# Loading four chunks ahead of the weights, transposing by DMA, and smaller first blocks in a fused retention and feed-forward kernel

## The chip, the core and the metric

The kernel runs on one core of a Trainium2 chip. The metric is device microseconds (us) from the first to the last instruction of the program, median over several executions. A program on one core is called "slow" here when it is over 1.5% above the fastest run of the same kernel; comparisons use fast runs. Every experiment was run in rounds with the kernel before on the same chip. Its medians in the rounds were 226.49, 225.42, 226.47 and 226.48 us, so differences between rounds of up to 1 us are not read as effects.

The engines are PE (matrix multiply, with PEld for its weight loads), DVE (vector), ACT (activation), POOL, and SP, which issues all DMA transfers of this kernel, in program order. Every engine is given its instructions in the order that the program fixed.

## The reference

Two stages. The first is a retention layer: 4 batches, 8 heads, 768 steps, head dimension 64. The second is a feed-forward layer with a squared ReLU on 3072 tokens.

```python
for t in range(S):                               # q, k, v: (4, 8, 768, 64) f32
    state = gamma * state + k[t] (x) v[t]        # per batch and head, 64 x 64
    y[t]  = scale * q[t] @ state
x = y.transpose(0, 2, 1, 3).reshape(3072, 512)
h = maximum(x @ w_in, 0)                         # w_in: 512 x 2048
out = (h * h) @ w_out                            # w_out: 2048 x 512
```

## The kernel before

The 768 steps of a batch are cut into 6 chunks of 128 steps, 24 chunks in all. For a chunk, k, q and v are loaded as f32 (256 KB each, in rows of 256 bytes), cast to bf16, and k and q are transposed. A "visit" on PE then computes the scores of a new chunk and the outputs of the chunk before it, from 64x64 matmuls. Its result `xt` is the input of the feed-forward: a first product (`ffn1`, with ReLU on ACT and squaring on DVE) and a second (`ffn2`), whose result is copied to `osb` and stored.

The kernel first builds a list of operations with assumed durations and dependencies, schedules it greedily (this part of the program is called the planner here), and then emits the instructions in that order. So a change of an assumed cost, a priority or a load order changes the order of the instructions on each engine, and that order is final.

```python
BLOCKS = [1, 1, 2, 2, 2, 4, 4, 4, 4]    # chunks that share one pass of the first product: 128, 256, 512 columns
PACE, LEAD = 6, 7                       # visits may run 7 chunks ahead of the feed-forward
ORDER = "p0 i0 i1 p1 i2 i3 o0 o1 o2 p2 o3"   # loads: p = two chunks, i/o = a quarter (1 MB) of w_in / w_out

# chunks 0..5: k, q of two chunks in one load of long rows, transposed row-wise (flip_rows),
#              k then transposed back (natural_keys)
# chunks 6..23: loaded singly, transposed one chunk ahead inside the visit:
def flips(m):
    for x, name in enumerate("kq"):
        for j in range(NJ):             # 4
            for sub in range(2):
                r = slice(L * sub, L * sub + L)
                for a in range(2):      # 32 transposes of 64x64 per chunk
                    nc.tensor.transpose(tpv[L*a : L*a+L, sub, 256*x + j*L : 256*x + j*L + L],
                                        bf[name][m % NBF][r, j, a, :], ident[r, r])
def evacuate(m):                        # one ACT copy, 128x1024, PSUM -> qkT
    nc.scalar.activation(qkT..., tpv..., AF.Copy)

def visit(m, n, t=None):                # m: outputs, n: scores, t: transposes
    def fn():
        if t is not None: flips(t)
        if m is not None: values(m); apply(m, 0); ...
        if n is not None: scores(n); sums(n)
        if m is not None: ...; apply(m, 1)
```

## Time and profile before

| what | value |
|---|---|
| median time | 226.32 us at first; 226.49 us over 4 runs beside the changed kernel |
| span of the profiled run | 225.5 us |
| PE busy | 204.8 us, 91% of the span |
| packet time of the DMA queue of the loads and stores | 58.8% of 16 engines' span |
| first matmul of the first product | 14.77 us |
| PE full from | about 44 us |

The page of the profile for the kernel before, cut to its summary: first the busy time per engine, then PE, granted clock and DMA in 40 slices of 5.6 us (a digit is a tenth, 9 is 90% or more), then the DMA queue, then the chain that ended last.

```profile
PE 204.8 (91%) x3210; PEld 116.0 (51%) x3236; DVE 112.7 (50%) x250; ACT 106.0 (47%) x168; POOL 39.0 (17%) x65
...
PE   4786778699999999999989999999999999999993
...
PEclk9997999999999999999999999999999999999999
DMA  6999999999999999998988510110011110111212
...
q1 hardware_dynamic: 70944, 33.56, 58.8%
...
PE 75%; SPq 11%; DMA 7%; issue 2%; ACT 2%; DVE 1%; POOL 0%; ACTq 0%; POOLq 0%
```

PE has nines from the ninth slice on; before it has 4 to 8, although the DMA is nearly full from the second slice on. So the first 44 us are limited by what has arrived, and the rest by PE itself.

The PE timeline of the kernel before, one visit in the full stretch (start us, duration us, engine, line, operation, out<-in, shapes, count), cut to its two groups of transposes, the matmuls after them, and the feed-forward that follows the visit:

```profile
98.38 0.32 PE L389 MATMUL yy<-ident,ks 64*64 64x64 bf16 x16
98.53 0.30 PE L389 MATMUL yy<-ident,qs 64*64 64x64 bf16 x16
98.65 0.30 PE L453 MATMUL yy<-pt,vs 64*64 64x64 bf16 x16
...
99.31 3.63 PE L593 MATMUL fps<-xt,w_in 128*128 128x512 bf16 x15
```

The 32 small transposes are the first two lines (L389). Each uses a 64x64 quarter of the 128x128 array, and their durations overlap: one starts every 8.4 ns (32 in 0.27 us), where a matmul of 128 columns that uses the whole array starts every 56 ns in this document's traces, so 28 ns would be its share for 64 columns (an estimate from these two figures). The whole visit takes 99.31 - 98.38 = 0.93 us.

### The profile page before, as it was taken

To read this page: it belongs to the slowest core of one execution; us is meant where nothing else is said; L and a number is where in the kernel's file an instruction comes from. 1 tells how busy PE (TensorE), PEld (TensorE's weight loads), DVE (VectorE), ACT (ScalarE), POOL (GpSimd) and SP (SyncE) were. 2 spreads that over 40 slices of the span, in tenths; PEclk is the share of its full clock that TensorE was granted. 3 is DMA by queue.
4 is the path that set the end of the run, shared out by engine and by line. 5 is a ranking of instruction groups with operands and counts; after the bars stand their busy time and mean duration, and the time that the engine had idled before them with its cause. 6 is when DMAs were issued, how large, how long until landed. Compare 5 with 4: busy or idle time off the path is not lost.

```text
span 225.5 us, 7244 instructions
## 1 busy us (share of the span) xinstructions
PE 204.8 (91%) x3210; PEld 116.0 (51%) x3236; DVE 112.7 (50%) x250; ACT 106.0 (47%) x168; POOL 39.0 (17%) x65
## 2 busy tenths in 40 slices
PE   4786778699999999999989999999999999999993
PEld 1545667554577875455545554444444444444441
DVE  1583955873188786699957765432222222220000
ACT  8315635644357552677555555434335444343121
POOL 3213224224323322332242200000000000000000
PEclk9997999999999999999999999999999999999999
DMA  6999999999999999998988510110011110111212
GB/s 150 265 337 189 337 376 237 184 346 197 283 211 200 236 187 213 231 202 179 206 188 177 146 49 3 47 49 12 35 47 47 49 47 1 47 49 47 93 49 91
DMA packets 70975, 34.02 MB, mean 151 GB/s; under 512 B 63008, under 2 KB 63008, under 8 KB 70944
## 3 DMA queue, kind: packets, MB, share of 16 engines
q1 hardware_dynamic: 70944, 33.56, 58.8%
q8 instruction: 25, 0.41, 0.8%
q14 instruction: 6, 0.05, 0.1%
HBM read 27.26 MB, written 6.29 MB: 149 GB/s over the span
## 4 chain that ended last, share of the span: by engine, by line
PE 75%; SPq 11%; DMA 7%; issue 2%; ACT 2%; DVE 1%; POOL 0%; ACTq 0%; POOLq 0%
PE fps L631 34%; PE fps L593 32%; DMA qn<-in_q_dram 7%; SPq L569 6%; SPq L362 4%; PE yy L389 3%; PE yy L468 2%; SPq L356 2%; PE yy L453 1%; ACT qkT L436 1%; PE sc L479 1%; PE sc L490 1%; DVE xt L555 1%; POOL qs L345 0%; PE yy L402 0%
## 5 line engine op out<-in xcount | busy, mean ns | idle before, releaser
L593 PE MATMUL fps<-xt,w_in 128*128 128x512 bf16 (+2 forms) x566 | 93.7, 309 | 3.9 <-POOL w_in L345 2.0
L631 PE MATMUL fps<-w_out,h 128*128 128x512 bf16 x368 | 90.1, 379 | 1.7 <-issue 1.3
L598 ACT ACTIVATE h<-fps 128x512 bf16<-128x512 f32 x96 | 56.6, 596 | 52.6 <-PE fps L593 51.5
L593 PEld LDWEIGHTS <-w_in 128*128 128x128 bf16 x576 | 50.5, 99 | 35.4 <-issue 2.1
L603 DVE TENSOR_TENSOR h<-h 128x512 bf16<-128x512 bf16 x96 | 42.4, 456 | 49.7 <-ACT h L598 49.5
L631 PEld LDWEIGHTS <-h 128*128 128x128 bf16 x384 | 36.7, 98 | 42.9
L555 DVE TENSOR_TENSOR xt<-yy,yf 128x512 bf16<-128x512 f32 x24 | 16.6, 690 | 21.6 <-ACT qkT L436 18.1
L436 ACT ACTIVATE qkT<-yy 128x1024 bf16<-128x1024 bf16 x18 | 18.4, 1023 | 18.2 <-PE yy L468 17.5
L639 ACT ACTIVATE osb<-fps 128x512 f32<-128x512 f32 x24 | 14.3, 597 | 21.7 <-PE fps L631 21.4
L377 DVE TENSOR_TENSOR vs<-vn,vf 128x512 bf16<-128x512 f32 x24 | 17.6, 735 | 4.8 <-DMA vn<-in_v_dram 4.8
L345 POOL CAST ks<-kn 128x512 bf16<-128x512 f32 x20 | 13.5, 677 | 35.0 <-DMA kn<-in_k_dram 19.8
L345 POOL CAST qs<-qn 128x512 bf16<-128x512 f32 x21 | 14.7, 701 | 27.3 <-DMA qn<-in_q_dram 27.3
L546 DVE TENSOR_TENSOR state<-sc,state 128x256 bf16<-128x256 f32 x40 | 16.7, 419 | 0.5
L533 DVE TENSOR_TENSOR pt<-sc,cmask 128x512 bf16<-128x512 f32 x24 | 16.3, 681 | 0.0
L468 PE MATMUL yy<-qkT,state 64*64 64x64 bf16 x352 | 12.5, 198 | 1.0 <-issue 0.6
L453 PE MATMUL yy<-pt,vs 64*64 64x64 bf16 x384 | 7.8, 195 | 2.8 <-DVE pt L533 1.4
L468 PEld LDWEIGHTS <-state 64*64 64x64 bf16 x352 | 7.6, 105 | 2.0 <-PE yy L468 1.1
L453 PEld LDWEIGHTS <-vs 64*64 64x64 bf16 x384 | 5.3, 107 | 5.5 <-issue 2.9
L479 PE MATMUL sc<-qkT 64*64 64x64 bf16 x384 | 7.9, 196 | 0.1
L341 ACT ACTIVATE w_in<-wst 128x512 bf16<-128x512 f32 x7 | 4.1, 623 | 7.7 <-DMA wst<-in_moe_w_in_dram 7.6
L490 PE MATMUL sc<-vs,ks 64*64 64x64 bf16 x352 | 7.6, 196 | 0.0
L693 PE MATMUL fps<-ident 128*128 128x512 bf16 x12 | 5.8, 605 | 1.6 <-POOL ident L297 1.6
(45 smaller groups left out, 85.0 us busy)
## 6 DMA issues: line engine op xcount, KB each, us to landing
vn<-in_v_dram SPq DMA_DIRECT2D x24, 256.0 KB, 5.9
out_dram<-osb SPq DMA_DIRECT2D x24, 256.0 KB, 2.0
kn<-in_k_dram SPq DMA_DIRECT2D x18, 256.0 KB, 5.5
qn<-in_q_dram SPq DMA_DIRECT2D x18, 256.0 KB, 5.7
wst<-in_moe_w_in_dram SPq DMA_DIRECT2D x4, 1024.0 KB, 9.7
wst<-in_moe_w_out_dram SPq DMA_DIRECT2D x4, 1024.0 KB, 10.5
kn<-in_k_dram SPq DMA_DIRECT2D x3, 512.0 KB, 11.6
qn<-in_q_dram SPq DMA_DIRECT2D x3, 512.0 KB, 13.4
```

The costliest lines, as they stand in the source:

```text
L345: nc.gpsimd.tensor_copy(o, t)
L377: lambda: nc.vector.tensor_tensor(out=o[:], in0=t.rearrange("s (h d) -> s h d", h=H), in1=vf[:, i, :, None].to_broadcast([P, H, D]), op=AL ...
L436: lambda: nc.scalar.activation(qkT.rearrange("p x j (s t) -> p s (x j) t", s=2), tpv.rearrange("p s (g t) -> p s g t", t=L), AF.Copy), pri ...
L453: nc.tensor.matmul(yy[L * c : L * c + L, sub, p * L : p * L + L], lhsT=vs[r, 4 * a + j, :], rhs=pt[r, a, j, :], start=(p == 0), stop=True, ...
L468: nc.tensor.matmul(yy[L * c : L * c + L, sub, p * L : p * L + L], lhsT=st[r, j, :], rhs=qkT[r, 1, j, sub * L : sub * L + L], start=False, ...
L533: lambda: nc.vector.tensor_tensor(out=pt[:], in0=sc[:, :, 0:256].rearrange("s g (p t) -> s g p t", p=NJ), in1=cmask[:, None, None, :].to_b ...
L546: f = lambda cc=cc, j1=j1, j0=j0: nc.vector.tensor_tensor(out=sts[j1][:], in0=cc, in1=sts[j0][:], op=ALU.add)
L555: lambda: nc.vector.tensor_tensor(out=xt[:, :, u * C : u * C + C].rearrange("s p (g t) -> s g p t", g=2), in0=yy[:, :, 0:256].rearrange("s ...
L593: nc.tensor.matmul(ps[:, u * n : u * n + n], lhsT=w_in_bf[j][:, cb, c * P : (c + 1) * P], rhs=xt[:, cb, cols], start=(cb == 0), stop=(cb = ...
L598: nc.scalar.activation(h2[:, f0 : f0 + per, cols], ps[:].rearrange("p (u n) -> p u n", u=per), AF.Relu)
L603: nc.vector.tensor_mul(hv, hv, hv)
L631: nc.tensor.matmul(ps[:], lhsT=h2[:, fb, u * C : u * C + C], rhs=w_out_bf[j][:, c, :], start=(fb == 0), stop=(fb == NFB - 1))
```

## The change

Its intent: fill the start of PE by loading four chunks before the weights, so that each weight quarter on arrival has four chunks to work on; take the transposes of chunks 8 to 23 off PE and off ACT by DMA transposes; and do the early transposes by whole 128x128 tiles. The planner is told that a DMA instruction holds SP (0.6 us for a load, 2.4 us for a transpose). The buffers for cast chunks and for transposed tiles go from four to five each. `F2LAG` sets how far the second product is planned behind the first. The diff, cut to its core, with comments added:

```diff
-BLOCKS = [1, 1, 2, 2, 2, 4, 4, 4, 4]
+BLOCKS = [1, 1, 1, 1, 1, 1, 2, 2, 2, 4, 4, 4]
-PACE = 6
-LEAD = 7
+PACE = 8
+LEAD = 2
+NPE = 6
+NTD = 8
-F2LAG = 5.0
+F2LAG = 3.0
-    NLD, NBF, NQT, ... = 4, 4, 4, ...
+    NLD, NBF, NQT, ... = 4, 5, 5, ...   # buffers: loaded, cast, transposed
-ORDER = "p0 i0 i1 p1 i2 i3 o0 o1 o2 p2 o3"
+ORDER = ("k0 q0 q1 v0 k1 q2 v1 k2 v2 v3 k3 q3 i0 i1 q4 o0 i2 i3 k4 o1 v4 o2 o3 v5 v6 q5 k5 q6 v7 q7 k6 k7")
...
-                eng_free[eng] = t + 0.08                  # planner: a DMA issue is nearly free for SP
+                eng_free[eng] = t + hold                  # planner: 0.6 us a load, 2.4 us a transpose
...
-    def flip_rows(m, x): ...                              # row-wise transposes of chunks 0..5
-    def natural_keys(m): ...
...
     def transpose(m):
+        if NPE <= m < NTD:
+            return                                        # chunks 6, 7: small transposes in a visit, as before
+        if m >= NPE:                                      # chunks 8..23
+            pl.add(f"X{m}", "SP", TURN, (f"bfk{m % NBF}", f"bfq{m % NBF}"), qkeys(m),
+                   lambda: nc.sync.dma_start_transpose(out=qkT.rearrange("p x j t -> p (x j) t"),
+                                                       in_=t.rearrange("s x j a d -> s (x j a d)")), prio=-0.5)
+            return
+        for x, name in enumerate("kq"):                   # chunks 0..5: 4 whole tiles each for k and q
+            ... nc.tensor.transpose(ps[:, j * P : j * P + P], t[:, x, j].rearrange("s a d -> s (a d)"), ident[:])
...
+            parts = 2 if q4 == NM - 1 else 1              # ffn2: the last token tile in two halves of 256 columns
...
-    (one chunk ahead: prepare(n + 1))
+        for x in range(0 if m < 0 else m + AHEAD, min(NM, m + AHEAD + 1)):   # AHEAD = 4
+            prepare(x)
+            transpose(x)
```

More of the change, by code (lines that the diff above doesn't have):

```diff
@@ L85, in schedule @@
         open_groups = set()
-        shared = [0.0, 0.0]
+        pipe = 0.0
         outstanding = {e: [] for e in eng_free}
@@ L116, in schedule @@
             if move:
+                cost, n_desc, hold = dur
                 out_ = outstanding[eng]
@@ L119, in schedule @@
                     out_.pop(0)
-                while sum(x[1] for x in out_) + dur[2] > self.RING:
+                while sum(x[1] for x in out_) + n_desc > self.RING:
                     t = max(t, out_.pop(0)[0])
@@ L130, in schedule @@
             if move:
-                dur, n_desc = (dur[:2] if t < 50 else dur[:1] * 2), dur[2]
-                eng_free[eng] = t + 0.08
-                for w in range(2):
-                    shared[w] = max(shared[w], t + self.DMA_LATENCY) + dur[w]
-                end[i] = max(shared) + self.LAND
-                out_.append((max(shared), n_desc))
-                dur = 0.08
+                eng_free[eng] = t + hold
+                pipe = max(pipe, t + self.DMA_LATENCY) + cost
+                end[i] = pipe + self.LAND
+                out_.append((pipe, n_desc))
+                dur = hold
             else:
@@ L153, in schedule @@
                         edge += self.BLOCK
-                        next_fetched = ahead + min(5.7, max(0.3, max(shared) - ahead)) + self.FETCH
+                        next_fetched = ahead + min(5.7, max(0.3, pipe - ahead)) + self.FETCH
                     issued += todo
@@ L175, in schedule @@
         return sorted(range(n), key=lambda i: (start[i], i))
-SMALL = (1.20, 1.55, 65)
-PAIR = (1.4, 1.6, 9)
-WIDE = (2.75, 2.75, 33)
-STORE = (0.72, 0.72, 9)
-BLOCKS = [1, 1, 2, 2, 2, 4, 4, 4, 4]
+SMALL = (1.20, 65, 0.6)
+TURN = (1.10, 16, 2.4)
+WIDE = (2.85, 33, 0.6)
+STORE = (0.80, 9, 0.6)
+BLOCKS = [1, 1, 1, 1, 1, 1, 2, 2, 2, 4, 4, 4]
 SPLIT = 6
+AHEAD = 4
 WARM = 20.0
 FILL = 0.8
-PACE = 6
-LEAD = 7
-NFP = 3
-F2LAG = 5.0
+PACE = 8
+LEAD = 2
+NPE = 6
+NTD = 8
+QACT = 0
+F2LAG = 3.0
 F2WAIT = 4
@@ L194 @@
 WPRIO = {"in": -2.0, "out": 2.0}
-ORDER = "p0 i0 i1 p1 i2 i3 o0 o1 o2 p2 o3"
+ORDER = (
+    "k0 q0 q1 v0 k1 q2 v1 k2 v2 v3 k3 q3 i0 i1 q4 o0 i2 i3 k4 o1 v4 o2 o3 v5 v6 q5 k5 q6 v7 q7 k6 k7"
+)
 def dma_order(nm):
-    seq = []
-    for t in ORDER.split() + [f"c{m}" for m in range(nm)]:
-        n = int(t[1:])
-        if t[0] == "p":
-            new = [("k", 2 * n), ("q", 2 * n), ("v", 2 * n), ("v", 2 * n + 1)]
-        else:
-            new = [(x, n) for x in "kqv"] if t[0] == "c" else [("in" if t[0] == "i" else "out", n)]
-        seq += [x for x in new if x not in seq]
-    return seq
+    names = {"i": "in", "o": "out"}
+    seq = [(names.get(t[0], t[0]), int(t[1:])) for t in ORDER.split()]
+    return seq + [(x, m) for m in range(nm) for x in "kqv" if (x, m) not in seq]
 @with_exitstack
@@ L246 @@
         assert 512 % (n * C) == 0 and x // 4 == (x + n - 1) // 4
-    NLD, NBF, NQT, NXT, NH2, NWS, NOSB, NST = 4, 4, 4, 4, 3, 4, 3, 6
+    NLD, NBF, NQT, NXT, NH2, NWS, NOSB, NST = 4, 5, 5, 4, 3, 4, 3, 6
     NBANK = 4
@@ L265 @@
     ld = {x: sb(f"{x}n", [P, NLD, H * D], FP32) for x in "qkv"}
-    bf = {x: [sb(f"{x}s{j}", [P, NJ, 2, D] if x != "v" else [P, H, D], BF16) for j in range(NBF)] for x in "qkv"}
+    kq = [sb(f"kqs{j}", [P, 2, NJ, 2, D], BF16) for j in range(NBF)]
+    bf = {"k": [t[:, 0] for t in kq], "q": [t[:, 1] for t in kq]}
+    bf["v"] = [sb(f"vs{j}", [P, H, D], BF16) for j in range(NBF)]
     qkts = [sb(f"qkT{j}", [P, 2, NJ, P], BF16) for j in range(NQT)]
@@ L352, in prepare @@
             t = ld[x][:, slot, :]
-            if x != "v" and m < 2 * NFP:
-                if m % 2 == 0:
-                    pl.add(f"ld{x}{m}", "SP", PAIR, (), (f"ld{x}{slot}", f"ld{x}{slot + 1}"),
-                           lambda x=x: nc.sync.dma_start(
-                               ld[x][:, slot : slot + 2, :].rearrange("s u n -> s (u n)"),
-                               src[x][b, :, i * C : (i + 2) * C, :].rearrange("h (w t) d -> w h (t d)", t=16)),
-                           prio=dma_prio[(x, m)])
-                continue
-            pl.add(f"ld{x}{m}", "SP", SMALL, (), (f"ld{x}{slot}",),
-                   lambda x=x, t=t: nc.sync.dma_start(
+            side = x == "q" and m < QACT
+            pl.add(f"ld{x}{m}", "ACT" if side else "SP", SMALL, (), (f"ld{x}{slot}",),
+                   lambda x=x, t=t, q_=nc.scalar if side else nc.sync: q_.dma_start(
                        t.rearrange("s (h d) -> s h d", h=H),
                        src[x][b, :, i * C : (i + 1) * C, :].rearrange("h s d -> s h d")),
-                   prio=dma_prio[(x, m)])
+                   prio=dma_prio[(x, m)] - 200 * side)
         for x in "kq":
             t, o = ld[x][:, slot, :], bf[x][m % NBF]
-            if m < 2 * NFP:
-                pl.add(f"c{x}{m}", CAST[x], 0, (f"ld{x}{slot}",), (f"bf{x}{m % NBF}",),
-                       lambda on, t=t, o=o: copy_on(on, o.rearrange("s j a d -> s (j a d)"), t), prio=urgency(m))
-                continue
             pl.add(f"c{x}{m}", CAST[x], 0, (f"ld{x}{slot}",), (f"bf{x}{m % NBF}",),
@@ L380, in prepare, with qkeys @@
                prio=urgency(m))
+    def qkeys(m):
+        return [f"qkT{m % NQT}.{x}" for x in "kq"]
     def flips(m):
@@ L390, in flips @@
                                             bf[name][m % NBF][r, j, a, :], ident[r, r])
-    def flip_rows(m, x):
-        to, key = (sc, "sc") if x == "k" else (yy, "yy")
-        for u in range(2):
-            bt = bf[x][(m + u) % NBF].rearrange("s j a d -> s (j a d)")
-            def fn(u=u, bt=bt):
-                for t in range(8):
-                    for a in range(2):
-                        nc.tensor.matmul(to[L * a : L * a + L, u, L * t : L * t + L], lhsT=bt[:, t * D : t * D + D],
-                                         rhs=ident.rearrange("p (w h) -> p w h", h=H)[:, :, NJ * a : NJ * a + NJ],
-                                         start=True, stop=True, skip_group_check=True)
-            pl.add(f"T{x}{m}.{u}", "PE", 0.35, (f"bf{x}{(m + u) % NBF}", "ident"), (f"{key}{u}",), fn,
-                   prio=-200 + m, lat=0.2, count=16)
-        cols = to.rearrange("p s n -> p (s n)").rearrange("p (t u w j) -> p u j w t", u=2, j=NJ, w=8)
-        for u in range(2):
-            o = qkts[(m + u) % NQT][:, "kq".index(x)].rearrange("p j (w t) -> p j w t", t=16)
-            pl.add(f"E{x}{m + u}", EVAC, 0, (f"{key}0", f"{key}1"), (f"qkT{(m + u) % NQT}.{x}",),
-                   lambda on, u=u, o=o: copy_on(on, o, cols[:, u]), prio=urgency(m + u), lat=0.05)
-    def natural_keys(m):
-        qkT, ks = qkts[m % NQT], bf["k"][m % NBF]
-        o1 = {}
-        def back():
-            ps = fps[o1["op"]["bank_index"]].bitcast(BF16)
-            for j in range(NJ):
-                nc.tensor.transpose(ps[:, j * P : j * P + P], qkT[:, 0, j, :], ident[:])
-        i0 = pl.add(f"B{m}", "PE", 0.24, (qkeys(m)[0], "ident"), (f"gB{m}",), back, prio=-200 + m, lat=0.2, count=4,
-                    bank=("open", ("B", m), False))
-        o1["op"] = pl.ops[i0]
-        pl.add(f"G{m}", EVAC, 0, (f"gB{m}",), (f"bfk{m % NBF}",),
-               lambda on: copy_on(on, ks.rearrange("s j a d -> s (j a d)"),
-                                  fps[o1["op"]["bank_index"]].bitcast(BF16)[:, 0:512]),
-               prio=urgency(m), bank=("close", ("B", m)))
-    def qkeys(m):
-        return [f"qkT{m % NQT}.{x}" for x in "kq"]
     def evacuate(m):
@@ L440, in transpose, with fn @@
     def transpose(m):
-        pl.add(f"T{m}", "PE", 0.45, (f"bfk{m % NBF}", f"bfq{m % NBF}", "ident"), ("yy0", "yy1"),
-               lambda: flips(m), prio=-200 + m, lat=0.2, count=32)
-        evacuate(m)
+        qkT, t = qkts[m % NQT], kq[m % NBF]
+        if NPE <= m < NTD:
[6 more added lines that the diff above has]
+        for x, name in enumerate("kq"):
+            o1 = {}
+            def fn(x=x, o1=o1):
+                ps = fps[o1["op"]["bank_index"]].bitcast(BF16)
+                for j in range(NJ):
+                    nc.tensor.transpose(ps[:, j * P : j * P + P], t[:, x, j].rearrange("s a d -> s (a d)"), ident[:])
+            i0 = pl.add(f"T{name}{m}", "PE", 0.26, (f"bf{name}{m % NBF}", "ident"), (f"gT{name}{m}",), fn,
+                        prio=-200 + m, lat=0.2, count=4, bank=("open", ("T", m, x), False))
+            o1["op"] = pl.ops[i0]
+            pl.add(f"E{name}{m}", EVAC, 0, (f"gT{name}{m}",), (qkeys(m)[x],),
+                   lambda on, x=x, o1=o1: copy_on(on, qkT[:, x].rearrange("p j t -> p (j t)"),
+                                                  fps[o1["op"]["bank_index"]].bitcast(BF16)[:, 0:512]),
+                   prio=urgency(m), lat=0.05, bank=("close", ("T", m, x)))
     def values(m):
@@ L521, in fn @@
                 apply(m, 1)
-        dur = 0.19 + (0.26 if m is not None else 0) + (0.26 if n is not None else 0) + (0.26 if t is not None else 0)
+        dur = 0.19 + 0.26 * ((m is not None) + (n is not None) + (t is not None))
         if n is None:
@@ L620, in ffn2 @@
             h2 = h2s[g % NH2]
-            grp = ("f2", q4)
-            o1 = {}
             slot = q4 % NOSB
-            for j in range(4):
-                reads = [f"h{g % NH2}.{u}.{4 * j + c}" for c in range(4)] + [f"wout{j}.{c}" for c in range(4)]
-                def mm(j=j, o1=o1, h2=h2, u=u):
-                    ps = fps[o1["op"]["bank_index"]]
-                    for c in range(4):
-                        fb = 4 * j + c
-                        nc.tensor.matmul(ps[:], lhsT=h2[:, fb, u * C : u * C + C], rhs=w_out_bf[j][:, c, :],
-                                         start=(fb == 0), stop=(fb == NFB - 1))
-                i0 = pl.add(f"F2.{q4}.{j}", "PE", 0.866, reads, (f"g{grp}",), mm,
-                            prio=(q4 + F2LAG) * 8 + 2 * j + 1, lat=0.2,
-                            bank=("open", grp, True) if j == 0 else ("use", grp), count=4)
-                if j == 0:
-                    o1["op"] = pl.ops[i0]
@@ L638, in ffn2 @@
-            pl.add(f"O{q4}", "ACT", 0.6, (f"g{grp}",), (f"osb{slot}",),
-                   lambda o1=o1, slot=slot: nc.scalar.activation(
-                       osbs[slot][:], fps[o1["op"]["bank_index"]][:], AF.Copy),
-                   prio=q4, bank=("close", grp))
-            pl.add(f"st{q4}", "SP", STORE, (f"osb{slot}",), (),
-                   lambda q4=q4, slot=slot: nc.sync.dma_start(out[rows(q4) : rows(q4) + C, :], osbs[slot][:]), prio=-1)
+            parts = 2 if q4 == NM - 1 else 1
@@ new lines, in ffn2, with mm @@
+            w = DM // parts
+            for part in range(parts):
+                ns = slice(part * w, part * w + w)
+                grp = ("f2", q4, part)
+                keys = [f"osb{slot}.{part}"] if parts > 1 else [f"osb{slot}.0", f"osb{slot}.1"]
+                o1 = {}
+                for j in range(4):
+                    reads = [f"h{g % NH2}.{u}.{4 * j + c}" for c in range(4)] + [f"wout{j}.{c}" for c in range(4)]
+                    def mm(j=j, o1=o1, h2=h2, u=u, ns=ns, w=w):
+                        ps = fps[o1["op"]["bank_index"]]
+                        for c in range(4):
+                            fb = 4 * j + c
+                            nc.tensor.matmul(ps[:, 0:w], lhsT=h2[:, fb, u * C : u * C + C], rhs=w_out_bf[j][:, c, ns],
+                                             start=(fb == 0), stop=(fb == NFB - 1))
+                    i0 = pl.add(f"F2.{q4}.{j}" + f"/{part}" * (parts > 1), "PE", 0.866 / parts, reads, (f"g{grp}",), mm,
+                                prio=(q4 + F2LAG) * 8 + 2 * j + 1 + part * 0.5, lat=0.2,
+                                bank=("open", grp, True) if j == 0 else ("use", grp), count=4)
+                    if j == 0:
+                        o1["op"] = pl.ops[i0]
+                pl.add(f"O{q4}" + f"/{part}" * (parts > 1), "ACT", 0.2 + 0.4 / parts, (f"g{grp}",), keys,
+                       lambda o1=o1, slot=slot, ns=ns, w=w: nc.scalar.activation(
+                           osbs[slot][:, ns], fps[o1["op"]["bank_index"]][:, 0:w], AF.Copy),
+                       prio=q4, bank=("close", grp))
+                pl.add(f"st{q4}" + f"/{part}" * (parts > 1), "SP", STORE, keys, (),
+                       lambda q4=q4, slot=slot, ns=ns: nc.sync.dma_start(out[rows(q4) : rows(q4) + C, ns], osbs[slot][:, ns]),
+                       prio=-1)
@@ L653 @@
         n = m + 1
-        early = n < 2 * NFP and n % 2 == 0
-        if early:
-            prepare(n)
-            prepare(n + 1)
-            flip_rows(n, "k")
-        elif 2 * NFP <= n <= SPLIT:
-            prepare(n)
-        if n < NM and n < SPLIT:
+        for x in range(0 if m < 0 else m + AHEAD, min(NM, m + AHEAD + 1)):
+            prepare(x)
+            transpose(x)
+        t = m + 2 if NPE <= m + 2 < NTD else None
+        if n < SPLIT:
             if m >= 0:
                 visit(m, None)
-            if early:
-                flip_rows(n, "q")
-                natural_keys(n)
-                natural_keys(n + 1)
-            elif n >= 2 * NFP:
-                transpose(n)
-            visit(None, n)
-        else:
-            if n == SPLIT:
-                transpose(n)
-            t = n + 1 if n + 1 < NM else None
-            if t is not None:
-                prepare(t)
-            visit(m if m >= 0 else None, n if n < NM else None, t)
+            visit(None, n, t)
+        else:
+            visit(m, n if n < NM else None, t)
         while done < NB and blk0[done] + blocks[done] - 1 == m:
```

## The prediction

> **What bounds the kernel now.** The page gives PE 204.8 of 225.5 us (91%); the chain of waits is 75% PE. From about 44 us on PE is full (busy-by-stretch view: 9.4 to 9.95 of every 10 us). Before that the chain is DMA and the SP queue (weights at 3.35, 16.31 and 21.6 us, q 25.69 for 16.6 us), with the DMA share near 1.0. From the PE timeline I count useful work: matmuls at 216 ns (512 columns), 112 ns (256) and 61 ns (128; 32 in 1.96 us), so about 85 us for the first product and 83 for the second; 0.93 us for a steady visit (98.38 to 99.31), some 31 us for visits and early transposes. Of 199 us in all, 24 lie before 44.5 us. The other 27 us are start, holes before 44 us, and a tail of 3.5 us.
>
> **What the change does, costed.**
> 1. The 32 small transposes of a visit take only 0.24 us of PE, start to start (102.87 to 103.11). 16 chunks lose them: -3.9 us on the critical path, since PE is full there. Their ACT evacuation (1.02 us each) goes too, but ACT is half idle.
> 2. Chunks 0 to 5: row-wise transposes (0.7 to 1.1 us per pair and tensor) and transposes back (0.6 us a pair) give way to 12 groups of four whole-tile transposes, about 0.25 us each: -4 us of PE work, in a stage only partly PE-bound.
> 3. Smaller blocks (chunks 2 to 5 from 256 to 128 columns, 8 to 11 from 512 to 256): +2 us on PE.
> 4. Start: twelve 256-KB loads precede the first weight. At the 190 to 200 GB/s that the slices show for such loads, they take 16 us; dense work starts near 23 us instead of 14.8. But then four chunks wait for every weight quarter (4 us of matmuls against 3 to 4 us of load), so PE stays full. At 44.5 us I expect 26 to 27 us of useful work done: -2.5 us.
> 5. DMA transposes move 256 KB each: at 190 to 220 GB/s, 1.2 to 1.35 us (estimate), the SP queue held perhaps 2 us. The Trainium skill (Advanced Engine Details and Errata, X-Bar Transpose) says they are as fast as regular DMAs; no run here shows it yet. With three loads (1.25 us each) a chunk needs about 5 us of DMA and of SP, against 7 to 8 us of PE: hidden.
> 6. The last token tile in two halves: -0.3 us.
>
> **Sum.** 226.3 - 3.9 - 2.2 (2 and 3 together) - 2.5 - 0.3 = about **217.5 us**, range 212.5 to 221.8. Chances: faster by over 2% 0.80, within 2% 0.14, slower 0.06.
>
> **What would show it.** First feed-forward matmul at 21 to 24 us, PE then nine tenths or more in every slice; steady visits near 0.68 us; no small transposes after chunk 7; PE busy down 5 to 8 us; no PE wait on transposed q and k over 0.5 us; DMA below full after 60 us.
>
> **What would make it wrong.** A DMA transpose that takes several times a plain copy, or holds SP so long that loads fall behind (PE would wait for the transposed tile from chunk 8 on); casts that come late and block the in-order SP queue; [...] weight quarters landing over 4 us apart, leaving holes between 23 and 50 us.

## The result

The changed kernel takes 216.48 us (215.83 to 216.62, 4 runs) against 226.49 us (225.99 to 227.60, 4 runs) for the kernel before. The ratio is 0.9546, with a 95% interval of 0.9505 to 0.9587. Ratios here are the mean time of one kernel's fast runs over that of the other's fast runs in the same rounds, so they are not quite the ratio of the quoted medians. The result is correct.

The page of the changed kernel, the same lines (slices of 5.4 us):

```profile
PE 200.8 (94%) x2764; PEld 119.8 (56%) x2764; DVE 115.4 (54%) x249; ACT 87.5 (41%) x145; POOL 39.9 (19%) x68
...
PE   6664899999999999999999999999999999999992
...
PEclk9965599999999999999999999999999999999999
DMA  7999999999999999989999999999811010011021
...
q1 hardware_dynamic: 99600, 37.76, 81.8%
...
PE 83%; DMA 6%; SPq 6%; ACT 1%; issue 1%; POOL 0%; DVE 0%; ACTq 0%
```

PE now has nines from the sixth slice on. The DMA queue's packet time rose from 58.8% to 81.8%, and the DMA row shows nines or eights until slice 28, about 150 us. The bytes of that queue rose from 33.56 to 37.76 MB; the difference, 4.2 MB, is 16 transposes of 256 KB.

The PE timeline of the kernel before at the start of the feed-forward (L593 is its first product; the brackets give idle time before the group and what ended it):

```profile
14.77 1.05 PE L593 MATMUL fps<-xt,w_in 128*128 128x128 bf16 x16 [0.48 <-DVE xt L555]
...
18.49 2.64 PE L593 MATMUL fps<-xt,w_in 128*128 128x128 bf16 x32 [2.01 <-POOL w_in L345]
...
41.23 0.69 PE L402 MATMUL sc<-ident,ks 128*64 128x64 bf16 x32 [2.56 <-POOL ks L345]
```

and of the changed kernel (L565 is the same product):

```profile
21.93 3.59 PE L565 MATMUL fps<-xt,w_in 128*128 128x128 bf16 x32 [0.62 <-POOL w_in L345]
...
26.32 1.96 PE L565 MATMUL fps<-xt,w_in 128*128 128x128 bf16 x32
...
28.34 7.31 PE L565 MATMUL fps<-xt,w_in 128*128 128x128 bf16 x128
35.49 0.39 PE L408 MATMUL fps<-ident,kqs 128*128 128x128 bf16 x4
```

The first product starts later (21.93 instead of 14.77 us), and from then on PE has no gap over 0.1 us until two waits of a quarter us near 86 and 91 us. Its first 32 matmuls take 3.59 us, the next 32 take 1.96: the clock row shows 5 tenths in slices 4 and 5, so the clock was halved there. The 128 matmuls from 28.34 to 35.49 take 56 ns each.

A visit of the changed kernel, in the same view, its first matmuls and the feed-forward that follows it:

```profile
79.54 0.32 PE L425 MATMUL yy<-pt,vs 64*64 64x64 bf16 x16
...
80.21 1.90 PE L608 MATMUL fps<-w_out,h 128*128 128x512 bf16 x8
```

The transposes are gone, and the visit takes 80.21 - 79.54 = 0.67 us.

### Where the time came from

How far the feed-forward has come can be counted from the traces without relying on modelled matmul ends. One evacuation of the first product by ACT stands for 4 matmuls of 512 columns, and one weight load of the second product for 1 (half a unit in the split last tile). The whole feed-forward is 768 such units of about 0.216 us. The table gives units begun by a time, and after the slash the number of chunks whose `xt` DVE has begun to write.

| us | 22 | 30 | 44.5 | 60 | 80 | 100 | 140 | 200 |
|---|---|---|---|---|---|---|---|---|
| before | 12/2 | 16/3 | 56/4 | 116/5 | 184/9 | 252/13 | 399/22 | 666/24 |
| changed | 0/3 | 20/4 | 80/5 | 148/5 | 220/9 | 296/12 | 462/18 | 722/24 |
| changed, blocks of before | 0/3 | 20/4 | 84/5 | 128/6 | 192/10 | 272/12 | 436/17 | 690/24 |
| changed, loads in the order of before | 16/2 | 16/3 | 76/4 | 124/5 | 196/9 | 272/12 | 438/17 | 695/24 |
| changed, first weight quarter earlier | 8/3 | 20/4 | 72/5 | 136/5 | 212/9 | 280/13 | 448/18 | 704/24 |
| changed, idle small transposes added | 0/3 | 24/4 | 88/5 | 148/5 | 216/9 | 296/12 | 450/18 | 704/24 |

The changed kernel is 12 units behind at 22 us, 24 units (5.2 us) and one visit ahead at 44.5 us, and 32 units (6.9 us) ahead at 60 us. At 200 us, when both have all visits behind them, it is 56 units (12.1 us) ahead, a count with steps of 4; the spans of the two profiled runs differ by 11.0 us. So a bit more than half of the gain is made by 60 us, and the rest while visits still run.

### The profile page after: what moved, and what is told of

The parts are those of the page before. It is cut to its first block, busy times and chain, and to the rows that moved or that the text cites. A ratio compares the mean times of both kernels' runs of the same rounds, so it can differ in the third digit from the quotient of the medians.

```text
span 214.5 us, 6317 instructions
## 1 busy us (share of the span) xinstructions
PE 200.8 (94%) x2764; PEld 119.8 (56%) x2764; DVE 115.4 (54%) x249; ACT 87.5 (41%) x145; POOL 39.9 (19%) x68
## 3 DMA queue, kind: packets, MB, share of 16 engines
q1 hardware_dynamic: 99600, 37.76, 81.8%
## 4 chain that ended last, share of the span: by engine, by line
PE 83%; DMA 6%; SPq 6%; ACT 1%; issue 1%; POOL 0%; DVE 0%; ACTq 0%
PE fps L608 38%; PE fps L565 38%; SPq L355 6%; DMA wst<-in_moe_w_in_dram 4%; DMA qkT<-kqs 3%; PE yy L425 2%; PE yy L440 2%; PE sc L451 1%; PE sc L462 1%; ACT qkT L387 0%; PE fps L408 0%; POOL w_in L345 0%; ACT osb L616 0%; PE yy L381 0%; DVE xt L527 0%
## 5 line engine op out<-in xcount | busy, mean ns | idle before, releaser
L565 PE MATMUL fps<-xt,w_in 128*128 128x128 bf16 (+2 forms) x768 | 94.0, 276 | 0.7 <-POOL w_in L345 0.6
L608 PE MATMUL fps<-w_out,h 128*128 128x512 bf16 (+1 forms) x400 | 92.2, 371 | 0.0
L565 PEld LDWEIGHTS <-w_in 128*128 128x128 bf16 x768 | 60.6, 100 | 29.1 <-POOL w_in L345 0.8
L616 ACT ACTIVATE osb<-fps 128x512 f32<-128x512 f32 (+1 forms) x25 | 14.5, 580 | 31.5 <-PE fps L608 30.4
L345 POOL CAST kqs<-kn 128x512 bf16<-128x512 f32 x24 | 15.9, 664 | 56.3 <-DMA kn<-in_k_dram 46.8
L345 POOL CAST kqs<-qn 128x512 bf16<-128x512 f32 x24 | 15.7, 654 | 37.5 <-DMA qn<-in_q_dram 37.5
L408 PE MATMUL fps<-ident,kqs 128*128 128x128 bf16 x48 | 5.6, 249 | 4.6 <-POOL kqs L345 4.6
L462 PE MATMUL sc<-vs,kqs 64*64 64x64 bf16 x352 | 7.9, 198 | 1.1 <-DVE vs L366 1.1
L341 ACT ACTIVATE qkT<-fps 128x512 bf16<-128x512 bf16 x6 | 3.6, 597 | 11.3 <-PE fps L408 11.3
L408 PEld LDWEIGHTS <-kqs 128*128 128x128 bf16 x48 | 3.4, 108 | 8.2 <-POOL kqs L345 7.7
```

What stands on the lines that cost most here:

```text
L345: nc.gpsimd.tensor_copy(o, t)
L565: nc.tensor.matmul(ps[:, u * n : u * n + n], lhsT=w_in_bf[j][:, cb, c * P : (c + 1) * P], rhs=xt[:, cb, cols], start=(cb == 0), stop=(cb = ...
L608: nc.tensor.matmul(ps[:, 0:w], lhsT=h2[:, fb, u * C : u * C + C], rhs=w_out_bf[j][:, c, ns], start=(fb == 0), stop=(fb == NFB - 1))
L616: lambda o1=o1, slot=slot, ns=ns, w=w: nc.scalar.activation(osbs[slot][:, ns], fps[o1["op"]["bank_index"]][:, 0:w], AF.Copy),
```

## Experiments

Twelve kernels ran, all with a correct result. The theory: (1) four chunks ahead of the weights and blocks of one chunk keep PE full from 22 us on; (2) the small transposes cost PE their start-to-start time, which the DMA transposes give back; (3) DMA transposes are hidden only if SP can issue them in time. The rivals: what the DMA transposes save they give back in contention; the start is the whole gain; or the order of loads hardly matters.

| run | median us | runs | ratio to before | 95% |
|---|---|---|---|---|
| changed kernel | 216.48 | 4 | 0.9546 | 0.9505 to 0.9587 |
| flips_late | 222.66 (one of 4 slow) | 4 | 0.9844 | 0.9763 to 0.9924 |
| pe_all | 227.56 | 4 | 1.0077 | 1.0011 to 1.0142 |
| dummy_flips | 221.71 | 6 | 0.9788 | 0.9744 to 0.9831 |
| before_dma | 229.08 | 4 | 1.0153 | 1.0097 to 1.0209 |
| before_dma_paced | 221.80 | 4 | 0.9811 | 0.9767 to 0.9856 |
| before_dma_honest | 228.07 | 4 | 1.0085 | 1.0037 to 1.0133 |
| old_pace | 216.15 | 4 | 0.9556 | 0.9519 to 0.9593 |
| old_blocks | 221.43 | 4 | 0.9825 | 0.9764 to 0.9885 |
| weights_early | 220.85 | 4 | 0.9764 | 0.9719 to 0.9809 |
| i0_earlier | 219.30 | 4 | 0.9687 | 0.9644 to 0.9730 |
| one_last | 215.19 | 6 | 0.9512 | 0.9479 to 0.9545 |
| serial_last | 215.48 | 6 | 0.9533 | 0.9498 to 0.9568 |

### What the small transposes cost on PE

Three runs ask this. The first sends chunks 8 to 23 back to the small transposes:

```diff
-NTD = 8
+NTD = 24
```

> The changed kernel with one constant moved (chunks 8 to 23 are transposed by the 32 small PE transposes inside the visit again, no DMA transposes). Theory A, the transposes cost PE their start-to-start time of 0.24 us a visit on the critical path: 216.5 + 16 x 0.24 = 220.3 us, steady visits near 0.92 us. Rival B, the DMA transposes give back in contention and waits what they save on PE: 216 to 217.5 us. Rival C, what counted was the 1.02 us ACT evacuation and its hold on the shared PSUM tile: 223 us or more, with waits of PE on that evacuation.

Its three fast runs took 220.76, 222.02 and 223.29 us, and the fourth, 224.13 us, counts as slow; that one was the profiled run, so its trace is not read here. The fast ones average 222.0 us, more than theory A's 220.3. Rival B (no change) is out. Rival C's 223 us or more lies above the mean, but one of the three runs reached it, and no fast run has a trace that could show waits on the evacuation. Between theory A and the reading that evacuations add something, this run does not decide, because the planner also moved other instructions.

The second adds the transposes and nothing else. They are computed in the same 16 visits and nobody reads them. The order on DVE, ACT, POOL and SP is the same as in the changed kernel, and PE differs only by the 512 added matmuls and their 512 weight loads:

```diff
-            reads += [f"bfk{n % NBF}", f"bfv{n % NBF}"] + qkeys(n)
+            reads += [f"bfk{n % NBF}", f"bfv{n % NBF}", f"bfq{n % NBF}"] + qkeys(n)
...
             if t is not None:
                 flips(t)
+            if n is not None and n >= NTD:
+                flips(n)
```

> The changed kernel with the 32 small PE transposes put back into the 16 visits from chunk 8 on, for no use: nobody reads them, the DMA transposes stay, and the order on every engine is the same but for them. Theory A: each costs its 0.24 us start to start and no more, 216.4 + 3.9 = 220.3 us; the rest of what flips_late lost (222.0 in its fast runs) is then its evacuations and the order of the loads. Rival B: the record times count, 32 x 0.19 us overlapping to 0.45 us a visit: 223.6 us. Rival C: PE has slack to hide them: 216 to 217.5 us.

It took 221.71 us (220.00 to 222.12), 5.2 us more than the changed kernel, or 0.33 us a visit. The PE timeline of this run:

```profile
80.54 0.45 PE L381 MATMUL yy<-ident,kqs 64*64 64x64 bf16 x32
80.81 0.30 PE L425 MATMUL yy<-pt,vs 64*64 64x64 bf16 x16
```

From start to start the transposes take 0.27 us, 16 x 0.27 = 4.3 us in all. The profiled run's span of 218.5 us is 4.0 us above that of the changed kernel, near theory A's 3.9, but the two traces do not start level: the first-product group after chunk 5 starts at 62.07 us here and at 62.94 us in the changed kernel, 0.87 us earlier, and the last matmul ends 3.95 us later. The stretch between is thus 4.8 us longer. The transposes are 4.4 us of it; a wait of 0.71 us at 70.23 us, whose cause the profile does not show, comes on top, and two waits of the changed kernel (0.48 us together, shown further down) are missing. That makes 4.6 us. The median is 1.2 us above the profiled run: the six runs lie between 220.00 and 222.12 us with no difference in clock that would sort them, and only one has a trace. How the start and the waits fell in the other five is open. Rival C is out, and rival B's 223.6 us lies above all six runs. The fast runs of flips_late are 0.3 us above in time (222.0) and 0.6% above by ratio, in other rounds and with another order, so what the ACT evacuation earned by itself is at most about 1 us and is not resolved.

The third run does all transposes by whole tiles on PE:

```diff
-NPE = 6
-NTD = 8
+NPE = 24
+NTD = 24
```

> The changed kernel with whole-tile PE transposes (8 per chunk, 128x128, through a PSUM bank and two copies) for all 24 chunks instead of only six. Theory A, all PE time after 22 us counts: 16 chunks x about 0.5 us + 2 x 0.25 us = +8.5 us, about 225 us, more than the small transposes cost because those run side by side in quarters of the array. Rival B, PE time of transposes hides: 217 us.

It took 227.56 us, over 2 us more than theory A's 225, and rival B is out. The PE timeline shows the cost (L408 is the transposes) and a second loss:

```profile
117.61 0.40 PE L408 MATMUL fps<-ident,kqs 128*128 128x128 bf16 x4 [0.76 <-POOL kqs L345]
...
122.26 0.40 PE L408 MATMUL fps<-ident,kqs 128*128 128x128 bf16 x4 [1.11 <-POOL kqs L345]
122.49 1.03 PE L608 MATMUL fps<-w_out,h 128*128 128x512 bf16 x4
123.36 0.39 PE L408 MATMUL fps<-ident,kqs 128*128 128x128 bf16 x4
123.58 2.75 PE L608 MATMUL fps<-w_out,h 128*128 128x512 bf16 x12
```

Four whole-tile transposes take 0.22 to 0.23 us from start to start, so the eight of a chunk take about 0.45 us. The 32 small ones move the same data in 0.27 us. And here PE reached a transpose before POOL had cast its input (0.76 us before 117.61 and 1.11 us before 122.26), which is part of the excess: the waits of PE on such casts are 6.6 us in sum here and 4.6 us in the changed kernel.

### When a DMA transpose is hidden

The next run puts DMA transposes, and nothing else, into the kernel before:

```diff
+                if t >= NTD:            # NTD = 8; the kernel before, one chunk ahead
+                    turned(t)           # dma_start_transpose on SP, in place of flips(t) and evacuate(t)
+                    t = None
             visit(m if m >= 0 else None, n if n < NM else None, t)
```

> The kernel before, with only one part of the change: chunks 8 to 23 get DMA transposes in place of the 32 small PE transposes, everything else as it was (planned one chunk ahead). Theory A, the parts add up: 226.5 - 3.9 = 222.6 us. Rival B, without the planning of chunks further ahead the DMA transpose comes too late and the visit waits for it: 225 us or more, with PE waits on the transposed tile of over 0.5 us.

It was slower than the kernel before: 229.08 us, ratio 1.0153, 3.7 us above the kernel before in the same rounds. Rival B holds. The waits of PE and PEld on the transposed tile in this run (line, what it waited for, us in total, times, longest):

```profile
PEld L489 <- DMA qkT<-kqs: 7.5, 10, 1.4
...
PE sc L489 <- DMA qkT<-kqs: 6.3, 9, 1.3
```

and the waits of SP itself on the cast that a transpose reads:

```profile
SPq L452 <- POOL kqs L349: 28.3, 14, 3.7
```

SP stood 28.3 us in front of 14 of 16 transposes. Its timeline shows why:

```profile
106.26 1.19 SPq L366 DMA_DIRECT2D kn<-in_k_dram  x1
107.50 1.10 SPq L366 DMA_DIRECT2D qn<-in_q_dram  x1
108.70 0.75 SPq L366 DMA_DIRECT2D vn<-in_v_dram  x1
109.55 2.21 SPq L452 DMA_TRANSPOSE qkT<-kqs  x1
111.82 0.57 SPq L366 DMA_DIRECT2D kn<-in_k_dram  x1
...
115.54 2.31 SPq L452 DMA_TRANSPOSE qkT<-kqs  x1
```

The order is k, q, v of one chunk and then the transpose of the chunk before it, over and over, with a store now and then and almost without a gap between the instructions. A transpose can go only when its own chunk's k and q have landed (median 4.7 and 4.5 us after issue in this run) and been cast. It comes to the head of the queue sooner than that, by 2.0 us on average (28.3 / 14), and until it goes SP, being in order, issues nothing. A chunk takes 6.0 us this way (109.55 to 115.54), and the next chunk's loads, and its transpose, start late in turn. PE's fixed order had the visits closer together than that (4.5 to 4.7 us in the kernel before), and PE waits inside them.

Two runs change when PE asks for the tile. One also lowers the lead of the visits:

```diff
-PACE = 6
-LEAD = 7
+PACE = 8
+LEAD = 2
-F2LAG = 5.0
+F2LAG = 3.0
```

> The kernel before with DMA transposes from chunk 8 on (as in the run before_dma) and, in addition, the visits' lead cut from 7 to 2 chunks ahead of the feed-forward (and the two constants that go with it). Theory A: before_dma lost because the visits ran at a pace of 5 to 6 us, faster than DMA can load and transpose a chunk; at the feed-forward's pace of 7 to 8 us PE no longer waits for the transposed tile, and the saving on PE shows: 222 to 224 us, PE waits on that tile under 2 us in total (7.5 before). Rival B: the DMA transpose is late whatever the pace: 228 to 229 us again.

221.80 us, ratio 0.9811: theory A. The waits of PE on the transposed tile shrink from 6.3 us to 0.8 us (2 waits, the longest 0.6 us; for the weight loads from 7.5 to 1.1 us), although SP still stands 22.0 us before 13 transposes. With more feed-forward between visits, the late tile is hardly waited for. Against the kernel before this is -4.7 us, close to what dummy_flips gives for the same 16 sets of small transposes (5.2 us). So the saving seems to be there once the wait is removed; but how much of the 4.7 us the shorter lead would earn without DMA transposes was not run.

The other leaves the lead at 7 and only tells the planner that a transposed tile lands later:

```diff
-                end[i] = max(shared) + self.LAND
+                end[i] = max(shared) + self.LAND + (1.5 if n_desc == 16 else 0.0)
```

> The run before_dma again, lead of 7 chunks as before, but the planner is told that a transposed tile lands 1.5 us later than it assumed, so that the fixed order of PE puts the visit later. Theory A: before_dma lost because PE's fixed order put visits ahead of their tile; with the later plan the waits on it shrink from 7.5 us to under 3 us, and the time falls to 222 to 225 us. Rival B: with a lead of 7 the DMA is simply too slow, wherever the planner puts the visits: 228 to 229 us.

228.07 us: theory A falls. PE's waits on the tile became fewer (5 instead of 9) but not shorter in sum (6.3 us for the matmuls, as before), and SP still waited 25.2 us. Assuming a later landing does not let SP issue more; that it is the rate that was short is my reading.

Then the same question in the changed kernel, with the lead put back to 7:

```diff
-PACE = 8
-LEAD = 2
+PACE = 6
+LEAD = 7
-F2LAG = 3.0
+F2LAG = 5.0
```

> The changed kernel with the visits' lead set back to 7 chunks (and its two companions back to the values of before). Theory A: PE waits for transposed tiles again, 3 to 8 us in total, 220 to 224 us. Rival B: four chunks of look-ahead in the loads are enough by themselves: 216 to 217.5 us.

216.15 us, ratio 0.9556: no difference. Rival B holds, and my expectation of 3 to 8 us of waits was wrong. The changed kernel does not need the shorter lead. Its SP timeline shows another order than before_dma:

```profile
92.61 2.32 SPq L355 DMA_DIRECT2D kn<-in_k_dram  x1
95.04 2.23 SPq L399 DMA_TRANSPOSE qkT<-kqs  x1
97.38 0.52 SPq L620 DMA_DIRECT2D out_dram<-osb  x1
98.00 1.28 SPq L399 DMA_TRANSPOSE qkT<-kqs  x1
99.33 0.57 SPq L355 DMA_DIRECT2D qn<-in_q_dram  x1
```

The fixed pattern is gone. Counting the loads ahead of them, the two transposes shown are those of chunks 13 and 14, and the k before them is that of chunk 15. So some transposes follow loads of two chunks later, and others (chunk 14 here) of one. SP waits on the casts for 15.5 us before 8 transposes (11.6 before 6 in old_pace), instead of 28.3 before 14. In addition the emitted order gives PE more feed-forward per visit: when 20 chunks had been visited, before_dma had done 400 units and old_pace 461. That the planner finds this order because it prepares four chunks ahead and charges SP for its holds is my reading of the diff. The fifth buffer for cast chunks and for transposed tiles, which before_dma does not have, may be needed for it as well. No run took these three apart.

### What the start depends on

```diff
-BLOCKS = [1, 1, 1, 1, 1, 1, 2, 2, 2, 4, 4, 4]
+BLOCKS = [1, 1, 2, 2, 2, 4, 4, 4, 4]
```

> The changed kernel with the blocks of before (two of 128 columns, three of 256, four of 512) instead of six, three and three. Theory A, the small blocks pay 2 us of PE work to keep PE full while the weights come: undoing them opens holes of more than 2 us between 22 and 55 us, 217 to 219 us. Rival B, the holes are filled by the second product anyway and the small blocks only cost: 214.5 us.

221.43 us: theory A in kind, but twice its size. The table of units shows no loss up to 44.5 us and 20 units lost (4.3 us) between 44.5 and 60 us. The PE timeline there:

```profile
46.60 2.75 PE L608 MATMUL fps<-w_out,h 128*128 128x512 bf16 x12 [0.91 <-POOL w_out L345]
...
57.70 0.45 PE L381 MATMUL yy<-ident,kqs 64*64 64x64 bf16 x32 [1.24 <-POOL kqs L345]
...
60.60 3.19 PE L565 MATMUL fps<-xt,w_in 128*128 128x256 bf16 x16 [1.89 <-DVE xt L527]
...
84.74 0.32 PE L451 MATMUL sc<-qkT 64*64 64x64 bf16 x16 [1.53 <-DMA qkT<-kqs]
```

Chunk 4 has been visited by 44.5 us, but it shares a block with chunk 5, whose visit comes near 58 us. Until then there is only second-product work, and it runs out: idle 0.91, 1.24 and 1.89 us, the last one for `xt`, plus a stretch at reduced clock after the gaps (16 matmuls of 256 columns take 3.19 us at 60.60, and 32 take 3.67 at 64.56). In all PE is busy for 12.05 of these 15.5 us, and for all 15.5 in the changed kernel. A block of one chunk can start as soon as that chunk is there. The last line shows a wait of 1.53 us on a transposed tile later on, in the re-planned order; it accounts for part of the rest.

Next, the loads in the order of before:

```diff
-    "k0 q0 q1 v0 k1 q2 v1 k2 v2 v3 k3 q3 i0 i1 q4 o0 i2 i3 k4 o1 v4 o2 o3 v5 v6 q5 k5 q6 v7 q7 k6 k7"
+    "k0 q0 k1 q1 v0 v1 i0 i1 k2 q2 k3 q3 v2 v3 i2 i3 o0 o1 o2 k4 q4 k5 q5 v4 v5 o3 v6 q6 v7 q7 k6 k7"
```

> The changed kernel with the loads in the order of before (two chunks, two weight quarters, two chunks, the other weights). Theory A: the first product starts near 15 us instead of 22, but holes open up to 45 us since only two chunks are there to use a weight quarter: 217.5 to 220 us. Rival B: work done before 22 us is pure gain, since PE is full afterwards: 212 to 215 us.

220.85 us, just above theory A's range; rival B is out. The row of the table tells it: 16 units done by 22 us and still 16 at 30 us. Two chunks use up what the first two quarters offer, and then PE waits for chunks and weights: it is busy for 4.10 of the 8 us from 22 to 30 us, and for 7.92 in the changed kernel. The order of the change has nothing done at 22 us and is ahead from 30 us on. But theory A's holes up to 45 us only use up the early lead: at 44.5 us this run is 4 units and one visit behind. Most of the loss comes after that (48 units from 44.5 to 60 us, against 68). Chunk 4, whose k and q now come behind three quarters of `w_out`, is visited at 47.70 us instead of 39.35, and then PE waits for the last quarter of `w_out`. Two of the waits:

```profile
28.31 3.57 PE L565 MATMUL fps<-xt,w_in 128*128 128x128 bf16 x32 [1.95 <-DVE xt L527]
...
51.28 1.02 PE L608 MATMUL fps<-w_out,h 128*128 128x512 bf16 x4 [1.43 <-POOL w_out L345]
```

Then a smaller step, the first quarter alone moved ahead of v2, v3, k3 and q3:

```diff
-    "k0 q0 q1 v0 k1 q2 v1 k2 v2 v3 k3 q3 i0 i1 q4 ...
+    "k0 q0 q1 v0 k1 q2 v1 k2 i0 v2 v3 k3 q3 i1 q4 ...
```

> The changed kernel with only the first weight quarter moved ahead of four loads (v2, v3, k3, q3). If work done before 22 us is pure gain, the 32 matmuls of chunks 0 and 1 on that quarter (2 us) come off: 214.5 us. If those holes are needed by the loads and the rest only shifts: 216 to 217 us.

219.30 us, 2.8 us worse, which neither of my lines covered. It is 8 units ahead at 22 us, even at 30, and 8 behind at 44.5. The chunks that came later leave gaps (PE is busy for 5.81 of the 8 us from 22 to 30 us), and the re-planned order also has one wait of 2.6 us on a transposed tile at 82.4 us:

```profile
82.40 0.32 PE L451 MATMUL sc<-qkT 64*64 64x64 bf16 x16 [2.61 <-DMA qkT<-kqs]
```

So about 1.7 us of the loss (8 units at 80 us) lies in the start; the wait, which comes from the planner's re-ordering, is more than enough for the rest.

### The last token tile

The prediction credited the split of the last tile with 0.3 us. In the changed kernel's trace both halves are evacuated back to back, because their matmuls alternate. The ACT group of the two halves and, below it, SP's two stores, which go out together:

```profile
206.32 4.09 PE L608 MATMUL fps<-w_out,h 128*128 128x512 bf16 x34
...
210.06 0.77 ACT L616 ACTIVATE osb<-fps 128x256 f32<-128x256 f32 x2 [2.46 <-PE fps L608]
```

```profile
210.47 0.81 SPq L620 DMA_DIRECT2D out_dram<-osb  x2
```

```diff
-            parts = 2 if q4 == NM - 1 else 1
+            parts = 1
```

> The changed kernel with the last token tile in one piece again. The trace of the changed kernel shows both halves' evacuations back to back at 210.06 us, because their matmuls interleave. Theory A: the split therefore gains nothing, 216.2 to 216.6 us. Rival B, as predicted: +0.3 us, 216.7 us or more.

```diff
-                                prio=(q4 + F2LAG) * 8 + 2 * j + 1 + part * 0.5, lat=0.2,
+                                prio=(q4 + F2LAG) * 8 + 2 * j + 1 + part * 8, lat=0.2,
```

> The changed kernel with the two halves of the last token tile one after the other on PE instead of interleaved. If the split is worth something only in this order, the first half's evacuation and store hide under the second half's matmuls, and the stretch from the last matmul to the end falls from 4.1 us to about 3.4 us: 215.8 us. If the store's fixed time rules: 216.4 us.

Without the split the kernel takes 215.19 us (214.82 to 215.86), and with the halves in sequence 215.48 us. The timeline of one_last at the end:

```profile
197.99 11.39 PE L608 MATMUL fps<-w_out,h 128*128 128x512 bf16 x51
...
209.46 0.60 ACT L616 ACTIVATE osb<-fps 128x512 f32<-128x512 f32 x1 [2.86 <-PE fps L608]
```

The tail, from the end of the last matmul to the end of the span, is 213.1 - 209.4 = 3.7 us without the split, 214.5 - 210.4 = 4.1 us with interleaved halves, and 213.5 - 209.7 = 3.8 us with halves in sequence, not the 3.4 us that I expected of these. So the split cost 0.3 us of tail instead of saving it. The other 1.0 us between the medians is not explained by the tail: up to the last tile the planned order on all engines is identical. In the profiled run of the changed kernel PE waits twice, 0.48 us together, on a transposed tile, and in that of one_last not at all; whether the split has any part in that is open. The two intervals (0.9479 to 0.9545 and 0.9505 to 0.9587) overlap, so one_last is at least as good as the changed kernel and clearly better than the kernel before. It is the version to keep.

## Why the prediction was right, point by point

The predicted 217.5 us lies 1.0 us from the measured 216.48, and the range held it. The mechanism was as described; the sizes of three terms were off, partly in opposite directions, so that the sum came this close is in part luck.

1. **Small transposes, -3.9 us.** Right in kind, too small. Visits did fall to 0.67 us as said, but taking the same work back in cost 5.2 us in the median (dummy_flips), and the same part alone in the kernel before earned 4.7 us (before_dma_paced). The prediction's 0.24 us (102.87 to 103.11) ends at the next weight load; the matmul after it starts at 103.14, and 0.27 us is what 16 of 18 visits show, which makes 4.4 us. The rest of the 5.2 us is waits and a start that was not level, as far as the one trace goes.
2. **Early transposes and 3. smaller blocks, -2.2 us together,** were not measured apart. Eight whole tiles take 0.45 us as assumed (four at about 0.25). What was missed is that the small blocks are no mere cost of 2 us: without them the kernel is about 5 us slower, since they are what lets PE stay full between 44.5 and 60 us.
4. **Start, -2.5 us.** The first product started at 21.93 us (21 to 24 predicted), and PE stayed full from there. Items 2 to 4 together were to give 4.7 us; measured are 24 units, 5.2 us, and one visit by 44.5 us, and 6.9 us by 60 us. The weight quarters were cast 2.8 to 4.8 us apart, once over the 4 us that the prediction called a danger, and that did not open holes.
5. **DMA transposes hidden.** Right for PE: two waits of 0.23 and 0.25 us in the whole trace. But "DMA below full after 60 us" was wrong: the DMA row stays at nines and eights until about 150 us. PE did not notice. The term that was mis-sized is the cost of a transpose: 1.2 to 1.35 us of DMA were assumed, and the queue's packet time gives 3.1 us (estimate, worked out in the last section). With three loads of 1.25 us a chunk then needs about 6.9 us of DMA instead of 5, only just under the 7 to 8 us of PE. The second danger that the prediction named, casts that come late and block the in-order SP, is exactly what made before_dma lose; the change is laid out so that it does not bite.
6. **Last tile, -0.3 us.** Wrong in sign: the halves interleave, and the tail grew from 3.7 us before to 4.1 us.

PE busy time was to fall by 5 to 8 us and fell by 4.0 us (204.8 to 200.8). This check was poorly chosen. The first 32 matmuls at half clock add 1.6 us after the change, and before the change 26 of 3236 matmuls have no record (3210 matmuls, 3236 weight loads), so that figure was too low. Start-to-start times and counts of evacuations were the better measure.

## What to carry to other kernels

- Before moving work off a full engine, read what it costs from start to start of its neighbours, not from the sum of its records; and then check the trace for who must now be in time. Sixteen DMA transposes saved about 5 us here, and lost 3.7 us in the kernel before, where each stood in an in-order queue, waiting for its cast, in front of loads that did not depend on it.
- Work done early is worth nothing if it only moves the hole. With full DMA at the start, load enough independent chunks that every weight piece, on arrival, has as much PE work as the next piece takes to load, and keep the blocks small enough that one late chunk does not hold back another.
- To split a last transfer, make sure that the halves do not finish together; otherwise the split only adds a store.

## What the Trainium skill lacked or had wrong

- **Advanced Engine Details and Errata, X-Bar Transpose (TRN2)** says that transposes by DMA are as fast as regular DMAs. From issue to landing that is nearly so here: median 4.6 us (3.0 to 6.5) for 256 KB, against 5.2 to 5.5 us for a plain load of that size. But adding 16 of them to the kernel before took the queue's packet time from 58.8% of 225.5 us to 80.0% of 227.3 us, that is 3.1 us of all 16 engines each (an estimate), and, if the other packets took what they took before, 46.6 ns per packet for the added 16,896 against 29.9 ns. And the instruction itself stood at SP for 1.24 to 4.42 us (median 1.88), where a load stands for 0.4 to 0.6 us when nothing holds it.
- **DMA: Bandwidth & Descriptors** does not say what a transpose between plain loads does to an in-order issuing engine when its source is not ready: 28.3 us of standing still in 14 of 16 cases (before_dma).
- **TensorE: Matmul & The Clock Gate, Back-to-back issue gap** gives sustained spacings of about 81 ns for 128 columns and 131 ns for 512 in a stream of weight loads and matmuls. Here 512 columns take 216 ns (16 in 3.46 us) and 128 columns take 56 ns (128 in 7.15 us), each matmul with its own weight load. (The first is read from the evacuations at 202.55, 206.01 and 209.46 us in one_last, 16 matmuls apart; the second from the PE timeline of the changed kernel, 28.34 to 35.49 us.) The same section's isolated form, N / 2.4 + 2.5 ns, fits both.
- **VectorE: DVE Perf Modes, The three transpose paths** lists 390 ns for one 128x128 transpose on PE and 1309 ns by DMA. In a stream, four on PE took 0.22 to 0.23 us, and eight by one DMA landed 3.0 to 6.5 us after issue. It does not list 64x64 transposes in quarters of the array, 32 of which moved as much data as eight such tiles in 0.27 us instead of 0.45.
